# A chain of attention and four matrix layers: the first two matrix layers by one level of Strassen, attention of all batches ahead of them, and SBUF laid out by hand

## The chip, the cores and the metric

The kernel runs on one core of one Trainium2 chip. The metric is the device time in microseconds (us), the median of several runs. The engines in this text: PE is TensorE (matmul; PEld is its weight load), DVE is VectorE, ACT is ScalarE, POOL is GpSimd, SP is SyncE, whose queue issues every DMA here.

## The reference

```python
# q, k, v: 4 batches, 12 heads, 448 positions, 64 wide
scores = q @ k.T / sqrt(64) - log(448)
x = sigmoid(scores) @ v                        # per head; joined to 1792 x 768
h = maximum(maximum(x @ w1, x @ w2), x @ w3)   # layer 1, 768 to 768
y = h @ w_out                                  # layer 2, 768 to 768
m = y @ w_in                                   # layer 3, 768 to 2048
out = (m * sigmoid(1.702 * m)) @ w_out2        # layer 4, 2048 to 768
```

q, k and v are float32. The weights arrive as the bits of float64 numbers, and the kernel rounds them itself.

## The kernel before, in words

**Precision.** PE reads float32 operands in a rounded form (`F32R`). To keep precision, an operand is split: `hi` is the rounded copy, made by a cast (`copy`, L228), and `lo` is the rest, made by a subtraction on DVE (`rest`, which goes through `two`, L231). A product of two split operands takes three matmuls: hi by hi, hi by lo, lo by hi (L385 to L387). Every matmul of the four layers multiplies a weight block of 128 by 128 with 448 columns, the positions of one batch.

**Stages.** A *pair* is two heads of one batch; there are 24. `Pair` loads q and k in one piece (`t`, 488 KB) and splits them (`qh`, `ql`). Scores come in four chunks of keys (`score`): chunks 0 to 2 hold two heads at once, chunk 3 is one matmul wide. ACT applies the sigmoid (`scored`, L445). Then the scores are weighed with v: the first ten pairs (`PLAIN`) in plain float32 (`weigh_plain`, L484), the others with scores and v split (`weigh`, L465 and L469). `unit1` and `unit2` are layers 1 and 2 for one batch and one block of 128 outputs: 18 matmuls into one bank of PSUM. Their 24 weight tiles are made once (`new_weights`): a DMA of 768 KB (`raw`), an ACT operation (L342) and four DVE operations (L349, L353, L354, L358; from the ninth tile on ACT does the second one's work at L347) round the float64 bits to float32, then the split. They are stored split in DRAM (`kept`) and loaded again for batches 1 to 3. `unit3` and `unit4` are layers 3 and 4 in 8 groups of 256 of the 2048 columns.

**Order.** The code hands every operation to a planner (`Order`) with an estimated duration and the parts that it reads and writes. PE's order is nearly the order of the calls; the planner fixes each engine's queue, and it chooses for a copy between ACT and DVE. After eleven *beats* of attention the main loop mixes: for each unit of layers 1 and 2 of a batch it calls a beat of attention of the next batches, so that attention is spread over the first three batches. Layers 3 and 4 follow. Buffers are rings of tiles in pools.

Of the kernel before, what the change touches and what calls it, by code (L numbers as in the profile page):

```python
# [25 lines left out]
QK = Q + S  # L26

OFF = 48
# [3 lines left out]
PLAIN = range(10)  # L32

LOW_ACT = range(8, NW1)
# [6 lines left out]


MM, SWITCH = 0.201, 0.41

SLACK = 12.0

# [13 lines left out]
class Ring:  # L60


    def __init__(self, n, make):
        self.n, self.make, self.tiles = n, make, []

    def tile(self):
        t = Tile(self)
        self.tiles.append(t)
        return t


class Tile:
    def __init__(self, ring=None, get=None):
        self.ring, self.get, self.ap, self.ops = ring, get, None, []

    def __call__(self):
        if self.ap is None:
            self.ap = self.ring.make() if self.ring else self.get()
        return self.ap

    def part(self, cut=None):
        return Part(self, cut)


class Part:


    def __init__(self, tile, cut):
        self.tile, self.cut, self.writers, self.readers = tile, cut, [], []

    def __call__(self):
        ap = self.tile()
        return self.cut(ap) if self.cut else ap
# [8 lines left out]
class Order:  # L102

    def __init__(self):
        self.ops, self.rings, self.clock = [], [], 0.0

    def ring(self, n, make, gate=None):
        r = Ring(n, make)  # L110
        r.gate = gate
        self.rings.append(r)
        return r

    def op(self, on, fn, reads=(), writes=(), after=(), at=None, lag=0.1):
        o = Op(len(self.ops), on, fn, at, lag)
        self.ops.append(o)
        for p in reads:
            o.pre.update(p.writers)
        for p in writes:  # L120
            o.pre.update(p.readers)
            o.pre.update(p.writers)
        for p in reads:
            p.readers.append(o)
            p.tile.ops.append(o)
        for p in writes:
            p.writers.append(o)
            p.tile.ops.append(o)
        o.pre.update(after)
        o.pre.discard(o)  # L130
        return o
# [6 lines left out]
    def run(self):  # L138
        for r in self.rings:
            for old, new in zip(r.tiles, r.tiles[r.n :]):  # L140
                first = min(new.ops, key=lambda o: o.n)
                first.pre.update(x for x in old.ops if x is not first)
            for t in r.tiles if r.gate else ():
                min(t.ops, key=lambda o: o.n).pre.add(r.gate)
# [30 lines left out]
        while len(done) < len(self.ops):  # L175
            for e in free:
                while free[e] <= now + 1e-9 and ready[e]:
# [4 lines left out]
                    o.fn(e)  # L182
                    if e == "SP":
# [19 lines left out]

def moe_chain_kernel(tc, qk, vv, wa, wb, out):
# [5 lines left out]
    def pool(name, bufs=1, **kw):  # L210
        return tc.alloc_tile_pool(name=name, bufs=bufs, **kw)

    def ring(p, name, shape, n, dtype=F32, gate=None):
        return O.ring(n, lambda: p[0].tile(shape, dtype, name=name, tag=name, bufs=n), gate)


    def dma(to, of, kb, reads, writes):
        return O.op({"SP": kb / 330.0}, lambda e: sp.dma_start(to().bitcast(F32), of().bitcast(F32)), reads, writes)
# [5 lines left out]

# [8 lines left out]
    def rest(to, of, hi, n):  # L233
        return two(to, of, hi, ALU.subtract, n)


    base = [pool("base", side="left")]
    att = [pool("att", side="left")]
    xp = [pool("xp", side="right")]
    mid = [pool("mid", side="right")]  # L240
    xe = [pool("xe", side="right")]
    scratch = pool("scratch", space=bass.MemoryType.DRAM)
    pmm = [pool("pmm", space=PSUM)]
    patt = [pool("patt", space=PSUM)]
    late, acc, pout = [None], [None], [None]

    def to_late(e):
        att[0].release()
        xe[0].release()
        patt[0].release()  # L250
        late[0] = pool("late", side="left")
        late[0].tile([P, 8], F32, name="space")
        pout[0] = pool("pout", space=PSUM)

    def to_acc(e):
        mid[0].release()
        xp[0].release()
        acc[0] = pool("acc", side="right")

    raws = ring(base, "raw", [P, DM], 2, mybir.dt.uint64)  # L260
    ys = ring(base, "y", [P, DM], 3)
    att_rings = [
        ring(att, *a)
        for a in (
            ("t", [P, 1024], 2),
            ("qh", [P, 1024], 2, F32R),
            ("ql", [P, 1024], 2, F32R),
            ("a2", [P, 2, S], 5),
            ("a1", [P, S], 2),
            ("ah2", [P, 2, S], 4, F32R),  # L270
            ("ah1", [P, S], 2, F32R),
            ("al2", [P, 2, S], 4, F32R),
            ("al1", [P, S], 2, F32R),
            ("vf", [P, 7, D], 1),
            ("vs", [P, 14 * D + 64], 2, F32R),
            ("vp", [P, 7, D], 2),
            ("xf", [P, S], 2),
            ("fold", [D, S], 2),
        )
    ]  # L280
    ts, his, los, a2s, a1s, ah2s, ah1s, al2s, al1s, vfs, vss, vps, xfs, folds = att_rings
    xs = [[ring(p, f"x{k}", [P, 2, S], 1, F32R) for k in range(KC)] for p in (xe, xp)]
    w1s = ring(xp, "w1", [P, 2 * DM + 64], 4, F32R)
    hs = [ring(mid, f"h{k}", [P, 2, S], 1, F32R) for k in range(KC)]
    mxs = ring(mid, "mx", [P, S], 2)
    yst = ring(mid, "yst", [P, 2, S], 3, F32R)

    def banks(p, name, n, shape=(P, 512)):
        return O.ring(n, lambda: p[0].tile(list(shape), F32, name=name, tag=name, bufs=n))

    scs, avs, mms = banks(patt, "sc", 2, (P, 2, 512)), banks(patt, "av", 2), banks(pmm, "mm", 2)
    pos = banks(pout, "po", 6)
    w2s = ring(late, "w2", [P, 2 * DM + 64], 7, F32R)
    z0s = [ring(late, f"z{k}", [P, 2, S], 2, F32R) for k in range(KC)]
    zs = [ring(acc, f"z{k}", [P, 2, S], B - 2, F32R) for k in range(KC)]
    gs = ring(late, "g", [P, 4 * S], 2, F32R)
    sgs = ring(late, "sg", [P, S], 2)
    gfs = ring(late, "gf", [P, S], 2)
    accs = ring(acc, "acc", [P, S], B * KC)

    bias = base[0].tile([P, 1], F32, name="bias")
    nc.gpsimd.memset(bias, -math.log(S))
    warm = yst.tile().part()
    O.op({"-": 0.0}, lambda e: nc.gpsimd.memset(warm().bitcast(F32), 0.0), [], [warm])
    warmed = base[0].tile([P, 1], F32, name="warmed")
    act.activation(warmed, bias, AF.Sigmoid)

    def dram(name, shape):
        return Tile(get=lambda: scratch.tile(shape, F32R, name=name)).part()

    kept = [dram(f"kept{i}", [P, 2, DM]) for i in range(NW1)]
    ykept = [[dram(f"yk{b}_{k}", [P, 2, S]) for k in range(KC)] for b in range(B)]

    def bank(r):
        return r.tile().part(lambda a: a[:, :S])

    def split(r):

        t = r.tile()
        return t.part(lambda a: a[:, 0]), t.part(lambda a: a[:, 1]), t  # L320

    def weight_tile(r):
        t = r.tile()
        of = lambda n: t.part(lambda a: a[:, OFF + n * DM :][:, :DM])
        return of(0), of(1), Part(t, lambda a: a[:, OFF:][:, : 2 * DM].rearrange("p (t n) -> p t n", t=2))

# [9 lines left out]
    def new_weights(of, hi, lo, of_n):  # L336
        raw, y = raws.tile().part(), ys.tile().part()
        O.op({"SP": 768 / 330.0}, lambda e: sp.dma_start(raw(), of), (), [raw])
# [11 lines left out]

        e = "ACT" if of_n in LOW_ACT else "DVE"
        O.op({e: 1.95 if e == "ACT" else 1.02}, lambda _: low(e), [raw], [raw])
# [9 lines left out]
        copy(hi, y, DM)  # L362
        rest(lo, y, hi, DM)

    def weights1(b, i):
        hi, lo, t = weight_tile(w1s)
        if b == 0:
            new_weights(wa[i], hi, lo, i)
            dma(kept[i], t, 768, [hi, lo], [kept[i]])
        else:  # L370
            dma(t, kept[i], 768, [kept[i]], [hi, lo])
        return hi, lo

    def weights2(i):
        hi, lo, _ = weight_tile(w2s)
        new_weights(wb[i], hi, lo, NW1 + i)
        return hi, lo

    def product(ps, w, x):
        for k, (hi, lo) in enumerate(x):  # L380
            c = slice(k * P, (k + 1) * P)

            def f(_, k=k, c=c, hi=hi, lo=lo):
# [10 lines left out]
    class Pair:  # L394
# [58 lines left out]
        def weigh(self, c):  # L453

            if self.av is None:
                self.av = [bank(avs) for _ in range(2)]
# [312 lines left out]
```

## Time and profile before

| what | value |
|---|---|
| three timed runs | 975.25, 977.39, 979.49 us (median 977.39) |
| span of the profiled execution | 975.8 us |
| instructions of PE, DVE, ACT | 4930, 914, 489 |
| moved by DMA | 165.36 MB, mean 169 GB/s |

The profiled execution is one run, looked at instruction by instruction. Its span, from the first to the last instruction, is 975.8 us; no time of its own is listed beside it, so it is set against the median of the timed runs, which is 1.6 us more. Busy time of an engine is given in us and as a share of the span.

### The profile page before, as it was taken

How to read it: one execution, taken by the hardware profiler on the slowest of the kernel's cores; microseconds unless marked ns; L12 is line 12 of the kernel's file. 1: busy time of each engine (PE TensorE's matmuls, PEld its weight loads, DVE VectorE, ACT ScalarE, POOL GpSimd, SP SyncE). 2: the span in 40 equal slices, each digit the busy share in tenths (PEclk: the TensorE clock that was granted, in tenths of full speed). 3: DMA queues.
4: the chain of work that ended last, by engine and by line, in shares of the span. 5: the costliest groups of instructions: out<-in, count | busy, mean ns of one | idle time of the engine just before them, and what ended most of it. 6: DMA issues, size and time to landing. Idle time of an engine off the chain costs nothing.

```text
span 975.8 us, 12162 instructions
## 1 busy us (share of the span) xinstructions
PE 961.8 (99%) x4930; PEld 855.1 (88%) x4930; DVE 596.4 (61%) x914; ACT 349.6 (36%) x489; POOL 1.1 (0%) x6
## 2 busy tenths in 40 slices
PE   7899999999999999999999999999999999999998
PEld 4457788888888889989999999999999999999997
DVE  6768799996667621521642555777757576754344
ACT  6666799754445420211212431222222122121110
POOL 0000000000000000000000000000000000000000
PEclk9999999999999999999999999999999999999999
DMA  8858887975555656799985021110201112000023
GB/s 293 304 195 288 298 300 265 401 280 203 191 188 195 196 187 211 287 360 359 328 318 226 20 68 63 65 65 17 80 33 65 65 65 65 1 1 1 1 104 123
DMA packets 39656, 165.36 MB, mean 169 GB/s; under 512 B 4400, under 2 KB 11056, under 8 KB 39600
## 3 DMA queue, kind: packets, MB, share of 16 engines
q1 hardware_dynamic: 39600, 164.58, 47.3%
q8 instruction: 39, 0.64, 0.3%
q14 instruction: 17, 0.14, 0.0%
HBM read 129.17 MB, written 35.39 MB: 169 GB/s over the span
## 4 chain that ended last, share of the span: by engine, by line
PE 92%; DMA 4%; DVE 2%; ACT 1%; issue 1%; SPq 0%; DVEq 0%; ACTq 0%
PE mm L385 19%; PE mm L387 19%; PE mm L386 18%; PE po L643 8%; PE po L642 8%; PE po L641 8%; PE sc L435 4%; PE av L465 3%; DMA raw<-in_wa 3%; PE av L484 3%; PE sc L437 1%; DMA w<-kept 1%; PE av L469 1%; ACT a L445 0%; ACT y L342 0%
## 5 line engine op out<-in xcount | busy, mean ns | idle before, releaser
L385 PE MATMUL mm<-x,w 128*128 128x448 f32 x432 | 158.6, 367 | 0.0
L386 PE MATMUL mm<-x,w 128*128 128x448 f32 x432 | 156.8, 363 | 0.9 <-DVE x L231 0.9
L387 PE MATMUL mm<-x,w 128*128 128x448 f32 x432 | 156.7, 363 | 0.0
L231 DVE TENSOR_TENSOR acc<-po,acc 128x448 f32<-128x448 f32 (+1 forms) x169 | 104.8, 623 | 59.8 <-PE po L643 59.1
L643 PE MATMUL po<-g,w 128*128 128x448 f32 x384 | 139.4, 363 | 0.0
L387 PE MATMUL mm<-z,w 128*128 128x448 f32 x384 | 139.4, 363 | 0.0
L642 PE MATMUL po<-g,w 128*128 128x448 f32 x384 | 139.2, 362 | 0.0
L386 PE MATMUL mm<-z,w 128*128 128x448 f32 x384 | 139.2, 362 | 0.0
L385 PE MATMUL mm<-z,w 128*128 128x448 f32 x384 | 138.2, 360 | 0.0
L641 PE MATMUL po<-g,w 128*128 128x448 f32 x384 | 138.2, 360 | 0.0
L625 ACT ACTIVATE sg<-mm 128x448 f32<-128x448 f32 x64 | 34.9, 545 | 245.0 <-PE mm L387 245.0
L445 ACT ACTIVATE a<-sc,bias 128x896 f32<-128x896 f32 (+1 forms) x96 | 84.8, 914 | 48.6 <-PE sc L435 36.9
L385 PEld LDWEIGHTS mm<-x,w 128*128 128x128 f32 x432 | 80.9, 187 | 13.6 <-issue 7.1
L231 DVE TENSOR_TENSOR mx<-mm,mx 128x448 f32<-128x448 f32 x48 | 29.9, 624 | 95.5 <-PE mm L387 95.3
L231 DVE TENSOR_TENSOR gf<-mm,sg 128x448 f32<-128x448 f32 x64 | 40.1, 626 | 77.2 <-ACT sg L625 77.0
L386 PEld LDWEIGHTS mm<-x,w 128*128 128x128 f32 x432 | 81.1, 188 | 6.7 <-DVE x L231 1.2
L387 PEld LDWEIGHTS mm<-x,w 128*128 128x128 f32 x432 | 81.0, 188 | 5.0
L642 PEld LDWEIGHTS po<-g,w 128*128 128x128 f32 x384 | 72.1, 188 | 5.7
L386 PEld LDWEIGHTS mm<-z,w 128*128 128x128 f32 x384 | 72.1, 188 | 5.7
L641 PEld LDWEIGHTS po<-g,w 128*128 128x128 f32 x384 | 71.8, 187 | 5.0
L385 PEld LDWEIGHTS mm<-z,w 128*128 128x128 f32 x384 | 71.8, 187 | 5.0
L387 PEld LDWEIGHTS mm<-z,w 128*128 128x128 f32 x384 | 72.1, 188 | 3.8
(78 smaller groups left out, 1334.2 us busy)
## 6 DMA issues: line engine op xcount, KB each, us to landing
w<-kept SPq DMA_DIRECT2D x72, 768.0 KB, 4.9
raw<-in_wb SPq DMA_DIRECT2D x32, 768.0 KB, 5.1
raw<-in_wa SPq DMA_DIRECT2D x24, 768.0 KB, 5.7
kept<-w SPq DMA_DIRECT2D x24, 768.0 KB, 5.3
t<-in_qk SPq DMA_DIRECT2D x23, 488.0 KB, 5.1
yk<-yst SPq DMA_DIRECT2D x24, 448.0 KB, 7.9
z<-yk SPq DMA_DIRECT2D x24, 448.0 KB, 7.3
out_t<-acc SPq DMA_DIRECT2D x23, 224.0 KB, 1.9
```

The lines of the kernel that those rows point to most:

```text
L231: return on("DVE", t_two(n), lambda: dve.tensor_tensor(to(), a(), b(), op=op), [a, b], [to])
L385: pe.matmul(ps(), wh[:, c], xh, start=k == 0, stop=False)
L386: pe.matmul(ps(), wh[:, c], lo(), start=False, stop=False)
L387: pe.matmul(ps(), wl[:, c], xh, start=False, stop=k == KC - 1)
L435: pe.matmul(o[:, e, :], kx[r, keys], qx[r, Q:QK], **how)
L445: on("ACT", t_act(n) + 0.07, lambda: act.activation(a(), ps(), AF.Sigmoid, bias=bias, scale=scale), [ps], [a])
L465: pe.matmul(av[e](), w, x()[:, e, :], start=c + n == 0, stop=False)
L484: pe.matmul(o[r], w, xe, start=c == 0, stop=c == 3)
L625: on("ACT", t_act(S), lambda sg=sg, ps=ps: act.activation(sg(), ps(), AF.Sigmoid, scale=1.702), [ps], [sg])
L641: pe.matmul(ps(), wh[:, c], gh, start=j == 0, stop=False)
L642: pe.matmul(ps(), wh[:, c], gl, start=False, stop=False)
L643: pe.matmul(ps(), wl[:, c], gh, start=False, stop=j == 1)
```

## The change

Five things change together.

**Strassen.** For layers 1 and 2 two batches are taken together, and the product is cut into blocks of two by two: weights into four quarters (`a11` to `a22`, 384 by 384), the moving side into half of the features by batch (`b11` to `b22`). Seven products (`product`, 9 matmuls each) replace eight, in Winograd's form. `moving` makes the seven moving operands by four subtractions (`combine`) and seven splits (`fill`); `Weights` makes the seven weight operands by four additions or subtractions and seven splits, in the first round only; the second round loads them from DRAM (`kept`, 384 KB each). A `Set` holds the seven products for one weight: three PSUM banks, in which sums grow, one ACT copy from bank to bank, two ACT copies to SBUF, and additions on the way out (`put`). `stage` interleaves the sets: step n of set i stands at 7i + 2n.

**Attention.** All 24 pairs come first, and all are weighed in plain float32. One weight tile is rounded per pair (`prepare`) and stored to DRAM as one float32 (`yk`, 384 KB); `LOW_ACT` is empty, so all four rounding operations stay on DVE.

**x, h and z** are kept as float32, and split where they are used. z of two batches goes through DRAM at 224 KB a piece.

**SBUF** is three slabs (`r`, `f`, `m1`, later `m2`) with fixed places, and dependencies by ranges of columns. **PSUM** is one tile of eight banks, handed out in turn.

```diff
-PLAIN = range(10)
-
-LOW_ACT = range(8, NW1)
+LOW_ACT = ()
...
+        def fill(self, base, cuts=((0, 2), (2, 1))):
+            for j, n in cuts:
+                split(self.parts(0, j, n), self.parts(1, j, n), F(base + j * T, n * T), n * T)
+
+        def pair(self, j):
+            return self.parts(0, j, 1), self.parts(1, j, 1)
+
+    def moving(base):
+        b11, b12, b21, b22, t = (base + 3 * i * T for i in range(5))
+        cuts = ((0, 2), (2, 1))
+
+        def combine(to, x, y):
+            for j, n in cuts:
+                sub(*(F(z + j * T, n * T) for z in (to, x, y)), n * T)
+
+        m = {k: Moving() for k in ("b11", "t1", "t2", "b21", "t3", "b22", "t4")}
+        m["b11"].fill(b11)
+        combine(t, b12, b11)
+        m["t1"].fill(t)
+        combine(b11, b22, t)
+        m["t2"].fill(b11)
+        m["b21"].fill(b21)
+        combine(b12, b22, b12)
+        m["t3"].fill(b12)
+        m["b22"].fill(b22)
+        combine(b21, b21, b11)
+        m["t4"].fill(b21)
+        return [m[k] for k in ("b11", "t1", "t2", "b21", "t3", "b22", "t4")]
...
+                y, s = yp_at(), s_at()
+                dma(F(y, 2 * DM), yk[i][0], 768)
+                q = [(y + n * HW) for n in range(4)]
+                self.s = [s + n * HW for n in range(4)]
+                a11, a12, a21, a22 = q
+                s1, s2, s3, s4 = self.s
+                self.steps = [
+                    (a11, None),
+                    (s1, (add, s1, a21, a22)),
+                    (s2, (sub, s2, s1, a11)),
+                    (a12, None),
+                    (s3, (sub, s3, a11, a21)),
+                    (s4, (sub, s4, a12, s2)),
+                    (a22, None),
+                ]
+
+        def operand(self, n):
+            at = w_at()
+            hi, lo, both = R(at + OFF, HW), R(at + OFF + HW, HW), R(at + OFF, 2 * HW)
+            k = kept[self.i][n]
+            if not self.first:
+                dma(both, k, 384)
+                return hi, lo
+            src, how = self.steps[n]
+            if how:
+                how[0](*(F(x, HW) for x in how[1:]), HW)
+            split(hi, lo, F(src, HW), HW)
+            dma(k, both, 384)
+            return hi, lo
...
+        O.pe(f, 9 * MM, [*w, *(z for p in parts for z in p)] + ([] if fresh else [ps]), [ps])
...
+        def step(self, n):
+            if n == 0:
+                self.w = self.weights()
+                self.a, self.b, self.e = (banks(ps_at()) for _ in range(3))
+            name = ("a", "e", "b", "a", "b", "e", "b")[n]
+            ps = getattr(self, name)
+            product(ps, self.w.operand(n), self.x[n], n < 2)
+            if n == 0:
+                copy(self.b, ps, S, psum=True, both=False)
+            elif n == 1:
+                self.m5 = temp()
+                copy(self.m5, ps, S, psum=True, both=False)
+            elif n == 2:
+                self.u2 = temp()
+                copy(self.u2, ps, S, psum=True, both=False)
+            elif n == 3:
+                self.put(0, 0, ps, None)
+            elif n == 4:
+                self.put(1, 1, ps, self.m5)
+            elif n == 5:
+                self.put(0, 1, ps, self.u2)
+            else:
+                self.put(1, 0, ps, None)
+
+    def stage(sets):
+        for _, s, n in sorted((7 * i + 2 * n, i, n) for i in range(len(sets)) for n in range(7)):
+            sets[s].step(n)
...
+        def weigh(self):
+            b, hp = divmod(self.p, NPAIR)
+            ps, v, a = banks(7), self.v, self.a
...
+                        wv, xe = (w[:, 2 * c + e], x[:, e * S : (e + 1) * S]) if c < 3 else (w[r, 6], x[r, :])
+                        pe.matmul(o[r], wv, xe, start=c == 0, stop=c == 3)
+
+            O.pe(f, 4 * 0.75 + SWITCH, [v, *a], [ps])
+            half, j = divmod(hp, HK)
+            base = XA if b < 2 else XB
+            copy(F(base + (6 * half + 3 * (b % 2) + j) * T, S), ps, S, psum=True)
...
+    def prepare(k):
+        for i, n, t in singles[k : k + 1]:
+            y = F(y_at(), DM)
+            single(wa[t], y, "DVE")
+            dma(yk[i][1](n), y, 384)
+
+    prev = None
+    for p in range(NP):
+        c = Couple(p)
+        if p == 0:
+            c.score(0, slice(0, 1))
+            c.score(1, slice(0, 1))
+            c.score(0, slice(1, 3))
+            c.score(1, slice(1, 3))
...
+            c.score(0)
+            c.score(1)
+        c.score(2)
+        c.score(3)
+        if prev:
+            prev.weigh()
+        prev = c
+        prepare(p)
+    prev.weigh()
...
+    def layer1(x, first):
+        sets = []
...
+                sets.append(Set(x, lambda m=m, e=e: Weights(3 * m + e, first), put))
+        stage(sets)
...
+    x = moving(XA)
+    for tp in range(2):
+        layer1(x, tp == 0)
+        h = moving(XA)
+        layer2(h, tp == 0, tp)
+        if tp == 0:
+            x = moving(XB)
+            for b in range(2):
+                for k in range(KC):
+                    dma(F(zf_at[b] + k * T, T), zk[b][k], 224)
...
-    for b in range(B):
-        first = at
-        for n, (layer, m, e) in enumerate(order):
-            while b < B - 1 and at < min(beats, first + -(-9 * (n + 1) // (17 if b else 22))):
-                beat(at)
-                at += 1
-            if (b, n) == (B - 1, len(order) - 1):
-                break
```

On PE, in the middle of attention, the rows before are these (`sc` are scores, `av` the weighed result, `vp` v, `mm` a bank of layer 1, `a` the sigmoids).

```order
L435 MATMUL sc<-qh,ql 128x448 x2
L484 MATMUL av<-a_568,vp 64x448 x2
L484 MATMUL av<-a_570,vp 64x448 x2
L484 MATMUL av<-a_594,vp 64x448 x2
L484 MATMUL av<-a_615,vp 64x448 x2
L437 MATMUL sc<-qh 128x448
L437 MATMUL sc<-ql,qh 128x448
L437 MATMUL sc<-qh,ql 128x448
L385 MATMUL mm<-x_308,w_313 128x448
L386 MATMUL mm<-x_308,w_313 128x448
```

At the end of attention the changed kernel has these on PE (L521 and L523 are scores, L550 weighs, L438 is a product of layer 1; `r`, `f`, `m` are the slabs, `ps` is PSUM).

```order
L521 MATMUL ps<-r 128x448 x18
L523 MATMUL ps<-r 128x448 x3
L550 MATMUL ps<-m_73,f 64x448 x8
L521 MATMUL ps<-r 128x448 x18
L523 MATMUL ps<-r 128x448 x3
L550 MATMUL ps<-m_73,f 64x448 x8
L438 MATMUL ps<-r 128x448 x9
L550 MATMUL ps<-m_73,f 64x448 x8
L438 MATMUL ps<-r 128x448 x558
```

No product stands between the scores of the pairs any more, and the first product of layer 1 stands ahead of the last weighing.

SP's queue in the middle of attention holds loads of q and k, of v and of `raw`, and stores of the split weights, in loose order before:

```order
L338 DMA raw<-in_wa 128x768
L412 DMA vp<-in_vv 128x448
L218 DMA kept_782<-w_749 128x1536
L338 DMA raw<-in_wa 128x768
L218 DMA kept_826<-w_801 128x1536
L404 DMA t<-in_qk 128x976
```

Now it repeats four DMAs per pair.

```order
L268 DMA f<-in_qk 128x976
L268 DMA f<-in_vv 128x448
L320 DMA f<-in_wa 128x768
L262 DMA yk_580<-f 128x768
L268 DMA f<-in_qk 128x976
L268 DMA f<-in_vv 128x448
L320 DMA f<-in_wa 128x768
L262 DMA yk_664<-f 128x768
```

The load of `raw` (L320) now stands behind the load of v, and the load of the next q and k behind the store of the rounded weight.

On DVE at the seam from layer 1 to layer 2 of the first round the changed kernel has these (L280 is every two-operand operation, L277 a cast or copy; `m_1272` is the slab `m2`, which holds the first moving operands of layer 2).

```order
L280 TENSOR_TENSOR f<-f 128x448
L280 TENSOR_TENSOR m_1272<-f,m_1272 128x896
L280 TENSOR_TENSOR f<-f 128x896
L280 TENSOR_TENSOR r<-f,r 128x384
L280 TENSOR_TENSOR f<-ps,f 128x448
L280 TENSOR_TENSOR f<-f 128x896
```

Two thirds of each moving operand (896 of 1344 columns) are made while layer 1 still runs; the last third follows when its last set is done.

## Rows read from the trace of the kernel before

**Rows 1.** The page's first part: busy time, share of the span, instructions.

```profile
PE 961.8 (99%) x4930; PEld 855.1 (88%) x4930; DVE 596.4 (61%) x914; ACT 349.6 (36%) x489; POOL 1.1 (0%) x6
```

**Rows 2.** Windows: stretch, its length, busy us (count) by engine, clock, DMA share, GB/s.

```profile
25.00:50.00 25.00, 21.59 (x115) 11.86 (x112) 18.08 (x26) 14.53 (x18) 0.00 (x0) 0.93 0.86 298
...
100.00:150.00 50.00, 49.49 (x257) 40.71 (x255) 43.65 (x65) 41.63 (x44) 0.00 (x0) 1.00 0.84 302
...
400.00:450.00 50.00, 48.92 (x245) 45.49 (x244) 19.88 (x30) 9.83 (x15) 0.00 (x0) 1.00 0.96 351
...
600.00:700.00 100.00, 100.00 (x502) 93.75 (x501) 70.25 (x113) 24.21 (x38) 0.00 (x0) 1.00 0.13 48
```

**Rows 3.** Timeline of PE: the first matmul of layer 3, the last of layer 4.

```profile
506.90 0.36 PE L385 MATMUL mm<-z,w 128*128 128x448 f32 x1
...
971.70 0.37 PE L643 MATMUL po<-g,w 128*128 128x448 f32 x1
```

**Rows 4.** The chain that ended last, 60 to 75 us: start, us, what.

```profile
61.34 1.41 PE sc L435 x12
...
67.98 3.31 PE av L484 x16
71.29 0.82 PE sc L437 x3
72.10 0.20 PE mm L385
```

**Rows 5.** Groups by line and shape, ACT: busy us, mean ns, idle before.

```profile
L445 ACT ACTIVATE a<-sc,bias 128x896 f32<-128x896 f32 x72 | 70.1, 1007 | 37.7 <-PE sc L435 36.9 <-PE av L484 0.5
...
L445 ACT ACTIVATE a<-sc,bias 128x448 f32<-128x448 f32 x24 | 15.2, 634 | 10.8 <-PE sc L437 10.7
...
L342 ACT ACTIVATE y<-raw 128x768 f32<-128x768 f32 x56 | 50.8, 913 | 50.8 <-DVE w L231 22.1 <-DMA raw<-in_wa 17.5 <-DMA raw<-in_wb 10.0
...
L228 ACT CAST x<-av 128x448 fp32r<-128x448 f32 x5 | 2.7, 533 | 6.3 <-PE av L484 6.3
```

**Rows 6.** Groups by line and shape, DVE.

```profile
L358 DVE SCALAR_TENSOR_TENSOR y<-raw,y 128x768 uint32<-128x768 uint32 x56 | 53.0, 959 | 1.0 <-ACT raw L347 0.3
...
L231 DVE TENSOR_TENSOR al<-a,ah 128x896 fp32r<-128x896 f32 x42 | 45.0, 1086 | 0.1
L349 DVE TENSOR_SCALAR raw<-raw 128x768 uint16<-128x768 uint16 x40 | 40.6, 1048 | 0.0
...
L353 DVE TENSOR_SCALAR y<-y 128x768 f32<-128x768 f32 x56 | 31.1, 557 | 9.7 <-ACT y L342 8.9
...
L354 DVE TENSOR_SCALAR y<-y 128x768 uint32<-128x768 uint32 x56 | 31.0, 566 | 0.1
L231 DVE TENSOR_TENSOR mx<-mm,mx 128x448 f32<-128x448 f32 x48 | 29.9, 624 | 95.5 <-PE mm L387 95.3
...
L231 DVE TENSOR_TENSOR ql<-t,qh 128x976 fp32r<-128x976 f32 x23 | 26.9, 1170 | 0.1
...
L228 DVE CAST qh<-t 128x976 fp32r<-128x976 f32 x14 | 9.3, 665 | 4.9 <-PE sc L437 4.8
```

**Rows 7.** Tile `raw`, 60 to 160 us: from issue to landing.

```profile
DMA to landing us min/median/max: 4.2/5.6/8.4
```

**Rows 8.** Timeline of ACT: the first two sigmoids.

```profile
7.29 1.90 ACT L445 ACTIVATE a<-sc,bias 128x896 f32<-128x896 f32 x2
```

**Rows 9.** Groups by line and shape: a copy out of PSUM by ACT.

```profile
L228 ACT COPY mx<-mm 128x448 f32<-128x448 f32 x14 | 7.6, 540 | 34.7 <-PE mm L387 34.7
```

**Rows 10.** Timeline of PE around a wait: start, us, what, idle time before.

```profile
38.28 0.48 PE L437 MATMUL sc<-qh 128*128 128x448 f32 x1 [2.00 <-ACT a L445]
...
41.23 0.58 PE L435 MATMUL sc<-ql,qh 64*128 64x448 f32 x2
41.61 0.58 PE L435 MATMUL sc<-qh,ql 64*128 64x448 f32 x2
42.12 4.16 PE L484 MATMUL av<-a,vp 128*64 128x448 f32 x16
```

More of the change, by code (lines that the diff above doesn't have):

```diff
@@ L245, in moe_chain_kernel @@
[L245 to L280, printed above, removed]
@@ L311, in moe_chain_kernel @@
[L311 to L325, printed above, removed]
+    XA, XB = 0, 15 * T
@@ L423, in score @@
[L423 to L430 removed]
+                tp, hp, lp = F(t + c.start, n), R(h + c.start, n), R(l + c.start, n)
+                load(tp, qk[p][:, c], n / 2)
+                copy(hp, tp, n)
+                sub(lp, tp, hp, n)
@@ new lines, in moe_chain_kernel, with put @@
+    prev.weigh()
+    gate[0] = O.op({"-": 0.0}, to_m2, after=set(s1.ops))
+    def layer1(x, first):
+        sets = []
+        for m in range(HK):
+            for e in range(3):
+                def put(half, tok, ps, other, m=m, e=e):
+                    to = F(XA + (6 * half + 3 * tok + m) * T, S)
+                    if e == 0 and other is None:
+                        copy(to, ps, S, psum=True)
+                        return
+                    if other is not None:
+                        new = to if e == 0 else temp()
+                        add(new, ps, other, S)
+                        ps = new
+                    if e:
+                        two(to, ps, to, ALU.max, S)
+                sets.append(Set(x, lambda m=m, e=e: Weights(3 * m + e, first), put))
+        stage(sets)
@@ new lines, in moe_chain_kernel, with layer2, put @@
+    zk = [[dram(f"z{b}_{k}", [P, S])[0] for k in range(KC)] for b in range(2)]
+    zf_at = [XB + 6 * T * b for b in range(2)] + [XA + 6 * T * b for b in range(2)]
+    def layer2(h, first, tp):
+        sets = []
+        for m in range(HK):
+            def put(half, tok, ps, other, m=m):
+                k = m + HK * half
+                to = temp() if tp == 0 else F(zf_at[2 + tok] + k * T, T)
+                if other is None:
+                    copy(to, ps, S, psum=True)
+                else:
+                    add(to, ps, other, S)
+                if tp == 0:
+                    dma(zk[tok][k], to, 224)
+            sets.append(Set(h, lambda m=m: Weights(9 + m, first), put))
+        stage(sets)
@@ L606, in moe_chain_kernel, with weights2 @@
+    w2_at = Round([WREG + i * 1600 for i in range(5)])
+    assert WREG + 5 * 1600 <= RW
+    def weights2(i):
+        at = w2_at()
+        y = F(y_at(), DM)
+        single(wb[i], y, "ACT" if i < 0 else "DVE")
+        hi, lo = R(at + OFF, DM), R(at + OFF + DM, DM)
+        split(hi, lo, y, DM)
+        return hi, lo
     NG = NF // 2
```

571 lines of the change are left out of this document (245 added, 326 removed).

## The prediction

> **What bounds the kernel now.** I read the page's busy shares first. PE is busy for 961.8 of 975.8 us, DVE for 61%, ACT for 36% [rows 1]. The windows say whether one engine holds this throughout. In 600 to 700 us PE is busy for all of 100.00 us at the full clock and DVE for 70.25; in 100 to 150, where attention and layer 1 are mixed, PE has 49.49 of 50, and DVE 43.65 and ACT 41.63 are close behind; only in 25 to 50 does PE show gaps (21.59 of 25) with a mean clock of 0.93 [rows 2]. So the end is set by the number of matmuls, except in the first 50 us. The timeline gives the price of one: from the first matmul of layer 3 at 506.90 to the last of layer 4 at 971.70 [rows 3] there are 2304 of layers 3 and 4 and the 18 of layer 2's last unit, so 2321 steps in 464.8 us, 0.2003 us each.
>
> From 506.90 to the end of the span are 468.9 us; less those 18 (3.6) layers 3 and 4 with the tail are 465.3. The other 1710 matmuls of layers 1 and 2 are 342.5. What is left, 975.8 - 468.9 - 342.5 = 164.4, is start, attention and waits.
>
> **Fewer products.** Layers 1 and 2 need 12 sets of 7 products of 9 matmuls, twice: 1512 in place of 1728. At 0.2003 that is 302.8 in place of 346.1: 43.3 us less, on the engine that is never idle there.
>
> **Attention by itself.** One pair on PE: two chunks of scores 1.41, the third 0.60 (three steps of 0.20), the narrow fourth 0.82, the plain weighing 3.31 [rows 4]: 6.14 us. The same pair asks of ACT three wide sigmoids, a narrow one, the first rounding step and the copy of x out of PSUM: 3 x 1.007 + 0.634 + 0.913 + 0.533 = 5.10 [rows 5]. Of DVE it asks the cast and rest of q and k and four rounding steps: 0.665 + 1.170 + 1.048 + 0.557 + 0.566 + 0.959 = 4.97 [rows 6]. Meanwhile x of the first two batches is made ready: 7 rests and 4 combinations, each 896 and 448 columns wide, 11 x (1.086 + 0.624) = 18.8 us of DVE [rows 6], some 0.85 per pair, and at most 7 x (1.007 + 0.634) = 11.5 of ACT, 0.5 per pair. So PE 6.14, DVE 5.8, ACT 5.6: PE still sets it, by little. DMA moves 488 + 224 + 768 + 384 = 1864 KB (1.91 MB) per pair, 311 GB/s at 6.14; the row of 100 to 150 has 302 at a share of 0.84 and that of 400 to 450 has 351 at 0.96 [rows 2], so a share of about 0.86.
>
> What may be slower is the chain of the weight tiles. Only two `raw` buffers exist, so a tile's load, ACT's step and DVE's four repeat every two pairs: 5.6 to land (median; up to 8.4) [rows 7], 0.91, 3.13, and in DVE's queue one cast and rest of q and k between them, 1.84: 11.5, or 14.3 with the slowest load, so 5.75 to 7.15 per pair before any waiting in the queues. SP's queue couples it to the pairs, since the next q and k wait behind `raw` and the store. PE's 6.14 is the floor; I take 6.4, near it: at this DMA share most loads should land as in the window of rows 7, a few late.
>
> The sum of the stage: ACT's first sigmoid starts at 7.29 [rows 8], as before, since the same loads come first; the first pair's sigmoids take 3.66, then come the second pair's last chunk (0.8) and the first weighing at a low clock (4.1, rows 10 have 4.16): 15.9. From there to the end of pair 22's weighing are 22 rounds of 6.4: 140.8, so 156.7. Then layer 1 needs its first operand. Before it stand the last tiles' steps on ACT and DVE, the store of tile 21, the load of the first rounded pair of tiles and a split. At 6.14 per pair, pair 21 starts at 15.9 + 19 x 6.14 = 132.6, its sigmoids end 0.6 + 3.66 later, and the copy of x, ACT's step and DVE's four take 0.53 + 0.91 + 3.13: 141.4. With 5.6 for the store and 5.6 for the load (both taken like `raw`) and 1.2 for the split that is 153.8, against PE free at 15.9 + 22 x 6.14 = 151.0: a wait of some 3, which moves with the pace. Then the last weighing, 3.4. Together 163.1, about what start, attention and waits take now (164.4): the plain weighing costs PE 3.31 against 14 steps of 0.20 for the split one, 0.5 more on 14 pairs, and DVE and ACT lose the splits of the sigmoids.
>
> **Seams and the first round of Strassen.** Per set DVE has 4 combinations and 7 rests of 384 columns, at most 0.624 each (the 448 row, [rows 6]), 6.9, and in layer 1 on average 4.7 exits of 0.624, 2.9: at most 9.8 in the 63 x 0.2003 = 12.6 us that PE needs. ACT has 3 copies of 0.54 [rows 9] and 7 casts of at most 0.634: 6.1. So PE sets the pace inside a layer. The copy from bank to bank has no row; the nearest is 0.54 out of PSUM [rows 9]. It must be done within one product, 1.8 us; from nothing to 1.8 it costs nothing, and I take nothing. Without that cover each 0.1 us would cost 24 x 0.1.
>
> At the seam to layer 2 the last thirds of the moving operands remain, 11 operations of 0.624. After the last product of layer 1 some six stand before the second operand (3.7 us) and PE has one product (1.8): 2 us, in each round. Layer 2 of round one also has to make x for round two: DVE needs 3 x 8.1 + 6.9 + 18.8 = 50 us, and PE gives 37.9 plus 12.6 of the next set: no room, so I put 4 there. The second set's weights wait for the store and load of the last tile, 11.2 us, with four products and a weighing (10.6) to cover it: 2. Together 10. The lower end is 2, if the planner's order hides all; the upper is 27, if at four seams nothing is hidden (4 x 6.9).
>
> The second round loads its 84 operands of 384 KB in some 155 us, 213 GB/s, under the rates above: nothing. Layers 3 and 4 keep their matmuls. They add 8 splits of z, 13.7 us of DVE, in the first groups, where DVE has some 30% free [rows 2]: nothing; without cover 13.7.
>
> **Sum.** 163.1 + 302.8 + 10 + 465.3 = 941.2 us of span. The profiled span stands 1.6 below the median of the runs shown, so **943**.
>
> One rule of the Trainium skill speaks against the change: "Perfetto Trace Analysis", section "Optimization Strategy", advises interleaving regimes with different bottlenecks, and the change takes apart what was interleaved. By it the attention stage should no longer run at PE's pace. The windows agree that the mixed stretch kept PE at 99% [rows 2]; by the sums above attention alone still leaves PE the longest, so I follow the sums and let the rule stand behind the first rival.
>
> **The rivals.**
> First, *the weight tiles set the pace of attention*: 7.0 to 7.6 per pair in place of 6.4, if loads land at 8 us. That is 22 x 0.6 to 1.2, 13 to 26 more: 956 to 969. For it: two buffers only, one in-order queue. Against it: the median landing. Its far end is the case on the other side: at 8.0 per pair, a chain of 16 us, the gain is gone, and each 1 us beyond costs 22; that asks for loads of over 9 us, beyond any in rows 7, or the ACT step queued behind a whole pair's sigmoids. At 8.5 the time is 989.
>
> Second, *nothing is lost*: 6.14 per pair, no wait at the end, seams of 2: 15.9 + 135.1 + 3.4 + 302.8 + 2 + 465.3 = 924.5, so 926.
>
> Third, *DVE sets the pace of round one*: if its queue order makes it wait on PE, 2 to 3 us more per set on 12 sets, 967 to 979.
>
> Fourth, *the clock falls in attention*. After 2.00 us of waiting the matmuls of a score came 0.38 apart, which is the lower of the clock's two levels (1.2 against 2.4 GHz), and the weighing took 4.16 in place of 3.31 [rows 10, 4], about 1.8 us lost each time. If every pair had such a wait it would be 22 x 3.5: 1020. In "TensorE: Matmul & The Clock Gate", section "The HAM clock gate", the skill says that the throttled clock is the default and activity releases it; the trace agrees with its 0.93 in the stretch with gaps [rows 2]. PE's queue in attention has no such gap if ACT's 5.6 fits under 6.14, so I give it little.
>
> That Strassen saves nothing is excluded by rows 1 and 3: matmuls stand back to back.
>
> **Chances.** Forecast (930 to 955) 0.60; nothing lost (922 to 930) 0.13; weight tiles up to 969 0.13, beyond 0.04; DVE in round one 0.06, half of it within 0.5% of now; clock 0.04. Under 0.5% (some 5 us) a measurement cannot tell a change from none. Faster by more: 0.60 + 0.13 + 0.12 + 0.03 = 0.88; within it 0.05; slower 0.07. The range for 8 in 10 is 924 to 967.
>
> **What would show it.** PE's matmuls fall by 216 in layers 1 and 2, with steps of 0.20 there. Weighings of attention come 6.1 to 6.7 apart; if they come at 7 or more, and ACT's first rounding step waits for `raw`, the first rival is right. The first product starts at 155 to 163. At the seams PE waits for rests by DVE, 2 to 4 us each. Layers 3 and 4 take 465 us. The prediction is wrong if attention ends after 170 or PE shows waits inside the sets.

## The result, and the profile after

The changed kernel takes 934.05 us (median; 933.24 to 935.65) beside 976.32 (973.67 to 979.49) for the kernel before on the same chip: a ratio of 0.957, 95% interval 0.9546 to 0.9594. The forecast was 943. The profiled execution is one of 933.24 us, with a span of 931.4.

The page's first part answers [rows 1]: PE has 216 matmuls less and is as full as it was.

```profile
PE 918.9 (99%) x4714; PEld 792.3 (85%) x4714; DVE 624.7 (67%) x987; ACT 351.9 (38%) x564; POOL 1.1 (0%) x6
```

All waits of PE in the changed kernel (what it waited for, us in total, times, longest) come to some 9 us, and only 3.6 of them stand at a product (L438):

```profile
PE ps L438 <- ACT r L277: 3.6, 1, 3.6
PE ps L566 <- POOL r L560: 1.7, 1, 1.7
PE ps L550 <- ACT f L277: 1.4, 1, 1.4
PE ps L521 <- ACT m L534: 1.0, 2, 0.8
PE ps L550 <- DVE f L277: 0.9, 1, 0.9
PE ps L521 <- DVE r L280: 0.3, 1, 0.3
```

The windows (columns as in [rows 2]) show attention at 15 to 156, the end of it, and the first sets of round one. DVE and ACT are high in attention but PE is higher; behind 167 PE has no gap, and DVE is busy 44.31 of 63.

```profile
15.00:60.00 45.00, 44.67 (x277) 22.87 (x277) 39.04 (x53) 34.51 (x46) 0.00 (x0) 1.00 0.84 295
60.00:110.00 50.00, 46.77 (x276) 22.37 (x274) 44.58 (x62) 40.17 (x53) 0.00 (x0) 1.00 0.83 286
110.00:156.00 46.00, 45.38 (x269) 21.63 (x265) 35.98 (x51) 34.10 (x45) 0.00 (x0) 1.00 0.87 301
156.00:167.00 11.00, 7.77 (x29) 4.29 (x30) 7.52 (x14) 4.25 (x10) 0.00 (x0) 0.84 0.62 246
167.00:230.00 63.00, 63.00 (x317) 59.05 (x316) 44.31 (x86) 27.55 (x57) 0.00 (x0) 1.00 0.91 319
```

PE's timeline has the weighings (L550), the first scores of a slow round, the first product (L438), and the first and last matmul of layers 3 and 4 (as [rows 3]):

```profile
42.88 3.38 PE L550 MATMUL ps<-m,f 128*64 128x448 f32 x16
49.00 3.38 PE L550 MATMUL ps<-m,f 128*64 128x448 f32 x16
...
61.25 3.38 PE L550 MATMUL ps<-m,f 128*64 128x448 f32 x16
65.39 2.67 PE L521 MATMUL ps<-r 64*128 64x448 f32 x18 [0.76 <-ACT m L534]
67.99 0.87 PE L523 MATMUL ps<-r 128*128 128x448 f32 x3
68.97 3.38 PE L550 MATMUL ps<-m,f 128*64 128x448 f32 x16
...
152.25 3.38 PE L550 MATMUL ps<-m,f 128*64 128x448 f32 x16
159.23 3.81 PE L438 MATMUL ps<-r 128*128 128x448 f32 x9 [3.61 <-ACT r L277]
162.97 3.38 PE L550 MATMUL ps<-m,f 128*64 128x448 f32 x16
...
465.19 0.36 PE L690 MATMUL ps<-r 128*128 128x448 f32 x1
...
927.59 0.37 PE L716 MATMUL ps<-m,r 128*128 128x448 f32 x1
```

An ordinary round, weighing to weighing, is 6.12 us (42.88 to 49.00). Five of the 22 are longer, by 5.9 us together: the first by 0.6, behind a wait for DVE's rest of q and k, the other four by 5.3; that of 61.25 takes 7.72. ACT's timeline says why there: the first rounding step (L324) waits 4.46 us for a raw tile, and the sigmoids (L534), whose scores are there, stand behind it in ACT's queue.

```profile
58.55 0.53 ACT L277 COPY f<-ps 128x448 f32<-128x448 f32 x1
63.54 0.90 ACT L324 ACTIVATE f<-f 128x768 f32<-128x768 f32 x1 [4.46 <-DMA f<-in_wa]
64.34 3.31 ACT L534 ACTIVATE m<-ps,bias 128x896 f32<-128x896 f32 x4
```

ACT waits for raw tiles six times in the stage, 17.0 us in all. What held this load back stands in the chain that ended last: DVE's last step on an earlier tile (L339) frees the buffer, and only then is the load issued.

```profile
54.44 0.97 DVE f L339
55.47 8.00 DMA f<-in_wa
```

For raw tiles the row that answers to [rows 7] (20 to 160 us, issue to landing) is a little later than before:

```profile
DMA to landing us min/median/max: 4.9/6.5/8.0
```

From the second product on (166.28, behind the last weighing) 765.1 us remain to the end of the span. That number is the measure of the experiments: what they change lies before that matmul or behind it.

### The profile page after: what moved, and what is told of

It is laid out like the page before. It is cut to its first block, busy times and chain, and to the rows that moved or that the text cites. A ratio compares the mean times of both kernels' runs of the same rounds, so it can differ in the third digit from the quotient of the medians.

```text
span 931.4 us, 12177 instructions
## 1 busy us (share of the span) xinstructions
PE 918.9 (99%) x4714; PEld 792.3 (85%) x4714; DVE 624.7 (67%) x987; ACT 351.9 (38%) x564; POOL 1.1 (0%) x6
## 4 chain that ended last, share of the span: by engine, by line
PE 83%; DMA 7%; DVE 6%; ACT 3%; issue 1%; SPq 0%; DVEq 0%; ACTq 0%
PE ps L438 33%; PE ps L716 8%; PE ps L692 8%; PE ps L691 8%; PE ps L715 8%; PE ps L714 8%; PE ps L690 8%; DMA f<-in_wa 4%; ACT m L534 2%; DMA f<-in_qk 2%; DVE r L280 1%; DVE f L339 1%; DMA yk<-f 1%; DVE f L331 1%; DVE r L277 1%
## 5 line engine op out<-in xcount | busy, mean ns | idle before, releaser
L280 DVE TENSOR_TENSOR f<-ps,f 128x448 f32<-128x448 f32 x305 | 188.0, 623 | 197.0 <-ACT f L696 76.4
L438 PE MATMUL ps<-r 128*128 128x448 f32 x1242 | 254.9, 364 | 3.6 <-ACT r L277 3.6
L438 PEld LDWEIGHTS ps<-r 128*128 128x128 f32 x1242 | 233.7, 188 | 21.3 <-ACT r L277 4.4
L280 DVE TENSOR_TENSOR r<-f,r 128x384 fp32r<-128x384 f32 (+4 forms) x246 | 179.5, 745 | 19.3 <-ACT r L277 16.2
L277 ACT CAST r<-f 128x384 fp32r<-128x384 f32 (+3 forms) x178 | 104.5, 609 | 97.7 <-DVE f L280 32.9
L277 ACT COPY f<-ps 128x448 f32<-128x448 f32 x113 | 60.4, 535 | 131.3 <-PE ps L438 106.3
L692 PE MATMUL ps<-r 128*128 128x448 f32 x288 | 104.5, 363 | 0.0
L716 PE MATMUL ps<-r 128*128 128x448 f32 x288 | 104.5, 363 | 0.0
L691 PE MATMUL ps<-r 128*128 128x448 f32 x288 | 104.4, 362 | 0.0
L715 PE MATMUL ps<-r 128*128 128x448 f32 x288 | 104.4, 362 | 0.0
L690 PE MATMUL ps<-r 128*128 128x448 f32 x288 | 103.7, 360 | 0.0
L714 PE MATMUL ps<-r 128*128 128x448 f32 x288 | 103.7, 360 | 0.0
L550 PE MATMUL ps<-m,f 128*64 128x448 f32 (+1 forms) x384 | 81.0, 551 | 2.4 <-ACT f L277 1.4
L534 ACT ACTIVATE m<-ps,bias 128x896 f32<-128x896 f32 x96 | 79.8, 924 | 1.8 <-PE ps L521 1.8
L280 DVE TENSOR_TENSOR f<-f 128x384 f32<-128x384 f32 (+2 forms) x104 | 66.5, 661 | 11.6 <-DMA f<-yk 11.2
L324 ACT ACTIVATE f<-f 128x768 f32<-128x768 f32 x56 | 51.1, 920 | 47.9 <-DVE r L280 22.9
L277 DVE CAST r<-f 128x976 fp32r<-128x976 f32 (+5 forms) x68 | 37.1, 550 | 45.9 <-PE ps L691 24.6
L550 PEld LDWEIGHTS ps<-m,f 128*64 128x64 f32 (+1 forms) x384 | 23.2, 135 | 49.1 <-issue 44.4
L331 DVE TENSOR_SCALAR f<-f 128x768 uint16<-128x768 uint16 x56 | 58.2, 1040 | 0.0
L438 PE MATMUL ps<-m,r 128*128 128x448 f32 x270 | 58.2, 362 | 0.0
L715 PEld LDWEIGHTS ps<-r 128*128 128x128 f32 x288 | 54.0, 188 | 4.2
```

Of the source, the lines that this page charges most:

```text
L277: return O.op(engines, lambda e: (act.copy if e == "ACT" else dve.tensor_copy)(to(), of()), [of], [to])
L280: return on("DVE", t_two(n), lambda: dve.tensor_tensor(to(), a(), b(), op=op), [a, b], [to])
L331: dve.tensor_scalar(half(2), half(1), 13, None, op0=ALU.logical_shift_right)
L438: pe.matmul(o, a[:, c], b, start=fresh and j == n == 0, stop=j == HK - 1 and n == 2, skip_group_check=True,)
L534: lambda: act.activation(to(), ps(), AF.Sigmoid, bias=bias, scale=scale),
L550: pe.matmul(o[r], wv, xe, start=c == 0, stop=c == 3)
```

## The experiments

Each run is compared with the changed kernel's 934.05 us; the ratio given is to the kernel before.

**Eight products.** The sets of layers 1 and 2 get the plain four blocks, two products each; attention, rounding and slabs stay.

```diff
-        for ... in sorted((7 * i + 2 * n, i, n) ... for n in range(7)):
+        for ... in sorted((8 * i + 2 * n, i, n) ... for n in range(8)):
-            name = ("a", "e", "b", "a", "b", "e", "b")[n]
-            product(ps, self.w.operand(n), self.x[n], n < 2)
+            half, k, tok = n // 4, n // 2 % 2, n % 2
+            product(self.c[tok], self.op, self.x[2 * k + tok], k == 0)
```

> Eight block products in place of seven in layers one and two, attention first and slabs as in the changed kernel. Theory (PE sets the pace everywhere, and the 216 matmuls that are gone are the whole gain): 216 x 0.2003 us come back, so 934 + 43 = 977 us, within 0.4% of the kernel before, and PE has no wait over 1 us at the seams. Rival 1 (attention apart, or the layout, gave part of the gain): 965 to 972. Rival 2 (attention apart costs, and the seven products gave more than their matmuls): 982 or more.

974.86 us (ratio 0.9983, interval 0.9969 to 0.9997): 40.8 more. The timeline splits it. The stretch behind the last weighing goes from 765.1 to 971.4 - 162.81 = 808.6, 43.5 more, the 216 steps. Ahead of it 3.5 us go, since the first weight operand is there in time and no gap opens.

```profile
162.81 12.48 PE L421 MATMUL ps<-r 128*128 128x448 f32 x60
```

So the theory holds, and all else that the change did (attention apart, plain weighing, slabs) comes to 0.2% with eight products.

**All weighings plain in the kernel before.**

```diff
-PLAIN = range(10)
+PLAIN = range(24)
```

> The kernel before, with all 24 batch pairs weighed in plain float32 instead of the first ten. Theory (PE sets the pace in the mixed rounds too): 14 weighings each about 0.5 us longer on PE, 7 us more, 981 to 985. Rival (the mixed rounds lose time on ScalarE and VectorE, which split the weights there, and plain weighing is part of the gain): 976 or less.

983.3 us (ratio 1.0086, interval 1.0064 to 1.0107), 7.0 more: the theory's number, and PE's busy time rises by 6.9, from 961.8 to 968.7. With e1_eight it says that the rest of the change beside Strassen (attention apart, the slabs, where x, h, z and the rounding lie) costs nothing together; it gives back about what the plain weighing takes. What each part does by itself is not shown.

**The raw loads cut short.**

```diff
+        k = slice(0, DM if loads[0] <= 2 or loads[0] > 24 else 96)
-        ... sp.dma_start(raw().bitcast(mybir.dt.uint64), of) ...
+        ... sp.dma_start(raw().bitcast(mybir.dt.uint64)[:, k], of[:, k]) ...
```

> In the attention stage each load of a raw weight tile brings one eighth of its bytes after the first two (the rest of the tile keeps what was there, so the output isn't the reference's); every instruction stands where it did. Theory (the five slow rounds, 5.9 us over the 22, come from raw tiles that land late, with ScalarE's first rounding step waiting ahead of the sigmoids): rounds of 6.12 throughout and an earlier first product, 5 to 9 us less, 925 to 929. Rival 1 (the slow rounds come from ScalarE's and VectorE's own work, 37 to 45 us of 50): 932 to 934. Rival 2 (they come from the stores of the rounded tiles and the loads of queries, keys and values): 931 to 934, with the waits then on these transfers.

922.58 us (ratio 0.9453, interval 0.9428 to 0.9479): 11.5 less, more than expected, since the gap before layer 1 went too. The rounds now take 6.12, but for the first (6.46). So the late raw tiles are the cause of the other slow rounds; ACT's and DVE's own work, which stayed, did not keep them slow. The shorter loads also bring the DMA share between 15 and 156 from 0.85 to 0.60, so this run does not part a buffer that comes free late from transfers that are slow; the next one does.

**Four raw buffers, three raw buffers.** Two slots of the moving ring lie in the slab that holds the sigmoids first, and that space takes two more raw buffers during attention.

```diff
-slots = [i * SLOT for i in range(7)] + [RW, RW + SLOT]
+slots = [i * SLOT for i in range(5)] + [RW + i * SLOT for i in range(4)]
...
+    raw_more = Round([F(a, 2 * DM) for a in raw_at.places]
+                     + [M1(14 * T + i * 1536, 2 * DM) for i in range(2)])
...
-        raw = F(at, 2 * DM)
+        raw = raw_more() if loads[0] <= 24 else F(raw_at(), 2 * DM)
```

> Four buffers for raw weight tiles in the attention stage instead of two (the two more lie in the slab of the sigmoids, made larger by two slots of the moving ring); order of the matmuls after attention as before. Theory (a tile of raw weights is late because its buffer comes free late): rounds of 6.12 and 4 to 7 us less, 927 to 930. Rival (the transfers themselves are the limit in that stage, 84% of the DMA engines' time): slow rounds remain, 932 to 934.

923.32 us (ratio 0.9462, interval 0.944 to 0.9483), 10.7 less, the fastest kernel here that computes the whole reference. Its PE has one wait in attention, of 0.77, and its timeline at the end of the stage shows rounds of 6.12 and the first product behind the weighing without a gap:

```profile
141.54 3.38 PE L552 MATMUL ps<-m,f 128*64 128x448 f32 x16
144.84 2.08 PE L523 MATMUL ps<-r 64*128 64x448 f32 x18
146.86 0.88 PE L525 MATMUL ps<-r 128*128 128x448 f32 x3
147.66 3.38 PE L552 MATMUL ps<-m,f 128*64 128x448 f32 x16
150.97 2.07 PE L440 MATMUL ps<-r 128*128 128x448 f32 x9
152.97 3.38 PE L552 MATMUL ps<-m,f 128*64 128x448 f32 x16
156.28 11.08 PE L440 MATMUL ps<-r 128*128 128x448 f32 x54
```

Behind 156.28 are 921.4 - 156.28 = 765.1 us, as in the changed kernel. Raw tiles land no sooner in this kernel (its page; KB each, median us to landing):

```profile
f<-in_wa SPq DMA_DIRECT2D x12, 768.0 KB, 7.0
m<-in_wa SPq DMA_DIRECT2D x12, 768.0 KB, 8.0
```

Against 6.6 in the changed kernel's page the medians are later, and ACT's rounding step waits for none. Between 15 and 156 the DMA engines move 329 GB/s, against 294. So the transfers were not the limit; that a load had to wait for one of two buffers was.

With `range(1)` in place of `range(2)` there are three:

> Three raw buffers instead of two (e10_raw4 had four). Theory (a buffer is held for the landing, 6 to 8 us, and the rounding, some 4 us, so a third already lets a round take 6.12): 923 to 925, like four buffers. Rival (four were needed): 926 to 930, with slow rounds left.

927.37 us (ratio 0.9498, interval 0.9473 to 0.9524): the rival's range. The trace keeps slow rounds, with one wait of 1.2 us on ACT's copy; three buffers get about two thirds of the gain of four.

**The weighing first, and another place for the last tiles.** Two edits on the 3.6 us gap before the first product. The first makes that product wait for the last weighing on PE; the second lets tiles 20 to 23 take two of the four places of the ring, so that the places of the first pair read back come free earlier.

```diff
+            first_after[0] = O.pe(f, 4 * 0.75 + SWITCH, [v, *a], [ps])      # weigh
...
-        O.pe(f, 9 * MM, [...], [ps])
+        O.pe(f, 9 * MM, [...], [ps], after)
```

> The last weighing is put ahead of the first product of layer one on PE; nothing else is meant to move. Theory: the weighing fills the 3.6 us in which PE waited for the first weight operand, the granted clock does not fall, and the first nine matmuls take 1.8 us and not 3.8; 3 to 5 us less, 929 to 931. Rival: the second operand (a sum on DVE and its split) is late in any case, so PE waits there: 1 us less at most, 933 to 934.

931.91 us (ratio 0.9552, interval 0.9537 to 0.9566), 2.1 less, between the two. The chain that ended last in this kernel shows the store of tile 21, then the load into its place, then ACT:

```profile
148.43 3.66 DMA yk<-f
...
152.15 5.22 DMA f<-yk
...
157.39 0.03 ACT r L277
...
157.81 0.53 ACT f L277
...
158.39 5.07 PE ps L554 x16
```

ACT waits for that load at the cast of the weight operand, and behind the cast stands the copy that frees the weighing's bank. So the weighing waits for the same load by another way, 2.97 us, and then takes 5.07 in place of 3.38; from 159 to 162 us the granted clock is 0.50.

```diff
-            y = F(y_at(), DM)
+            y = F(y_at.places[k % 4 if k < 20 else 2 + k % 2], DM)
```

> The last four rounded tiles use two of the four places of their ring, so that the first pair of tiles read back for layer one no longer waits until the tile before last is stored. Theory (the 3.6 us wait before the first product, and the low clock behind it, come from that place alone): the load is issued some 10 us earlier, the first operand is there when attention ends, the gap and the slow first product go: 4 to 6 us less, 928 to 930. Rival (two places for the last four tiles delay their rounding, or VectorE has no time for the operand): 932 to 935, the wait then on VectorE.

927.41 us (ratio 0.9503, interval 0.9478 to 0.9529), 6.6 less. The first product follows the weighing at once, in 2.08 us in place of 3.81. By the profiled spans it is 4.4 less, all of it ahead of the last 765.1 us. The weighing behind that product now waits 0.74. So the gap came from that place, which comes free late. Another place is not the only cure: e10_raw4 and e6_short_raw leave the places as they were, their raw tiles do not come late, and no gap opens there either.

**A rounding step back on ACT.**

```diff
-            single(wa[t], y, "DVE")
+            single(wa[t], y, "DVE" if k < 8 else "ACT")
```

> The changed kernel with one rounding step of the raw tiles from the ninth on put back on ScalarE (1.95 us there, 1.03 us on VectorE). Theory (ScalarE then has 5.2 + 1.95 = 7.1 us of work in a round of 6.1 to 6.4 and sets the pace): 11 to 16 us more, 945 to 950. Rival (casts and evictions that may run on either engine go to VectorE instead, and ScalarE keeps 6.2 us a round): 934 to 938.

933.44 us (ratio 0.9556, interval 0.9528 to 0.9585): no difference that can be measured. My theory fell, and the rival's mechanism is there: between 15 and 156 us ACT's casts drop from 12 to 4 and its copies from 20 to 8, which DVE takes, and ACT's busy time rises by 11.6 us only. The move of this step, part of the change, is worth nothing here.

**The seams.** The moving operands made in one piece, with the changed kernel's attention and then with four raw buffers:

```diff
-        def fill(self, base, cuts=((0, 2), (2, 1))):
+        def fill(self, base, cuts=((0, 3),)):
...
-        cuts = ((0, 2), (2, 1))
+        cuts = ((0, 3),)
```

> The moving operands of each layer are made in one piece of three tiles, not in two tiles and then one. Theory (the seams cost nothing because two thirds of each operand are made ahead, and only one tile's work stands behind the last set): PE waits 1 to 3 us for the second or third operand at each of the two seams into layer two, 2 to 6 us more, 936 to 940. Rival (the three products left in the last set are cover enough whatever the cut): 934 as before, no wait over 0.5 us.

> e10_raw4 with the moving operands made in one piece of three tiles: the seams by themselves, since with four raw buffers the attention stage has no stalls that could move. Theory (e4_whole's 7.1 us more were the seams): 5 to 7 us above e10_raw4, 928 to 930, waits at the seams into layer two alone. Rival (half of e4_whole's loss was the end of the attention stage): 2 to 4 us more, 925 to 927.

941.13 us (ratio 0.9646, interval 0.9624 to 0.9668), 7.1 more; and with four buffers 931.6 (0.9537, interval 0.9513 to 0.9561), 8.3 above e10_raw4 (9.1 by the spans), both more than their theory gave. The second product of layer 1 divides them: from it on are 6.6 us more than the 765.1 in the first and 930.5 - 160.49 = 770.0, 4.9 more, in the second. The 1.7 between them stand behind the second seam, where PE waits 1.80 in both: in e4_whole the granted clock is 0.50 behind it (440 to 442 us), in e13_raw4_whole it stays at 1.00. In e13_raw4_whole the other 4.2 lie in attention, where around 42 us ACT's rounding step waited twice for a store to free its place (1.94 and 1.90 us), the copy that frees a weighing's bank stood behind it, and PE idled 2.72. The waits stand at the two seams into layer 2, and nowhere else in layers 1 and 2 (timeline of PE in e13_raw4_whole; a fifth, of 0.25, is at 424.43):

```profile
270.95 5.68 PE L440 MATMUL ps<-m,r 128*128 128x448 f32 x27 [0.17 <-DVE m L280]
277.43 3.68 PE L440 MATMUL ps<-m,r 128*128 128x448 f32 x17 [0.80 <-DVE m L280]
...
285.30 10.87 PE L440 MATMUL ps<-r 128*128 128x448 f32 x53 [0.39 <-DVE r L280]
...
431.90 3.68 PE L440 MATMUL ps<-r 128*128 128x448 f32 x17 [1.80 <-DVE r L280]
```

What in the planned order hides them was the last question: at the seam into layer 2 of round one the planner puts set two's first product and set one's fourth, both ready early, ahead of set one's second.

```diff
...
+            after = third if n in (0, 3) else []
-            product(ps, self.w.operand(n), self.x[n], n < 2)
+            o = product(ps, self.w.operand(n), self.x[n], n < 2, after)
+            if n == 2 and not third:
+                third.append(o)
...
```

> e10_raw4, in which the first three products of each layer's first set stand ahead of the first product of the second set and of the fourth product (in the changed kernel the planner puts these two, whose operands are ready early, between the first product and the second). Theory (these two products, 3.6 us of PE, are what hides the last third of the second operand at the seams into layer two): PE waits 1 to 3 us for a rest by VectorE at each of these two seams, 2 to 6 us more than e10_raw4, 925 to 929. Rival (the two-thirds cut alone is enough): 923 to 924, no wait there.

924.11 us (ratio 0.9469, interval 0.9456 to 0.9482), 0.8 more than e10_raw4 and no wait of a product listed: the rival. In this kernel's timelines, PE and then DVE, the 36 matmuls from 264.75 are the last two products of layer 1, then the first and second of layer 2. They take 0.4 us more than 36 steps.

```profile
264.75 7.76 PE L440 MATMUL ps<-m,r 128*128 128x448 f32 x36
272.36 3.76 PE L440 MATMUL ps<-r 128*128 128x448 f32 x18
```

```profile
266.75 0.62 DVE L280 TENSOR_TENSOR f<-ps,f 128x448 f32<-128x448 f32 x1
...
267.76 0.62 DVE L280 TENSOR_TENSOR f<-f 128x448 f32<-128x448 f32 x1
...
269.10 1.62 DVE L280 TENSOR_TENSOR f<-f 128x448 f32<-128x448 f32 x3
270.63 0.62 DVE L280 TENSOR_TENSOR r<-f,r 128x448 fp32r<-128x448 f32 x1
271.17 0.62 DVE L280 TENSOR_TENSOR m<-f,m 128x448 fp32r<-128x448 f32 x1
```

The quarter that the second operand needs leaves the product before the last (ends at 266.55); its maximum is the first row, its combination with the first quarter the second, its rest the last, done at 271.79. Only the rest of the last tile comes so late, and a product reads that in its eighth matmul, which starts at 271.84. Until then PE has the last product of layer 1, the first of layer 2 and seven steps of the second, 1.8 + 1.8 + 1.4 = 5.0 of the 5.2 us.

**One product fewer.**

```diff
-            product(ps, self.w.operand(n), self.x[n], n < 2)
+            w = self.w.operand(n)
+            if n != 4:
+                product(ps, w, self.x[n], n < 2)
```

> The fifth product of each set of layers one and two is left out (216 matmuls fewer, so the output isn't the reference's); its operands are still made, stored and read, and all sums on VectorE stay. Theory (PE is still what bounds these layers, with VectorE busy 44 us in 63 in the first set): 43 us less, 889 to 893. Rival (VectorE's or ScalarE's sums and splits, or the 90% busy DMA engines, are close behind and bind in round one): 25 to 38 us less, 896 to 909, with PE waits inside the sets of round one.

895.39 us (ratio 0.9173, interval 0.914 to 0.9206; runs from 891.83 to 898.11), 38.7 less: at the border of the two. The profiled run is the fastest of them, 41.4 us below the changed kernel by the spans. Behind its first product PE now waits five times, 3.5 us in all: four times in round one (2.75 us, for ACT's and DVE's operands, 1.09 at most) and once, 0.75, for a load of `kept`, which stands in round two. So at six products PE still sets nearly all of the time, but the others are close; what the slower runs lose besides is not shown.

## Why the prediction was right, and where its size was off

The mechanism held: the gain is 216 matmuls at 0.20 us, and attention apart costs about what it did mixed. By the sum's terms:

- **Start and attention**: 163.1 foretold. The second pair's last chunk and the first weighing end at 14.96 (15.9; the weighing took 3.38, at the full clock). The 22 rounds end at 155.56, 6.39 each (6.4). The wait is 3.61 (3), and the product behind it 1.9 us slower at a granted clock of 0.84 in that window, which I had not counted. Less the first product's ordinary 1.8 the stage ends at 164.5, 1.4 late.
- **1512 products**: 302.8 foretold. From 164.5 to layer 3's first matmul at 465.19 are 300.7 us, in which 1503 stand (nine of the last set come later), 0.2001 each.
- **Seams**: this is the step that failed. I put 10: 2 at each seam into layer 2, 4 at x for round two and 2 at the second set's weights. The steps above leave nothing for any of them: 0.0. "After the last product of layer 1 some six stand before the second operand (3.7 us) and PE has one product (1.8)" had the wrong start and too little cover: the operand hangs on the product before the last, and only its last tile is late, the rest of which PE reads after seven steps of the product. Hence 5.0 of cover, even without the two products that the planner puts there (e14_strict). For x in round two I had "no room", 50 us of DVE in 50.5; the rows below show DVE busy for 34.71 in the 38 us of layer 2, and for 13.41 in the 38 behind it. The lower end, "if the planner's order hides all", was the place to stand; the 2/1 cut carries it (4.9 us more without, 6.6 where the clock fell), the order of the products gives at most 0.8. What covers the second set's weights no run takes apart.

```profile
280.00:318.00 38.00, 38.00 (x192) 35.62 (x191) 34.71 (x57) 22.69 (x43) 0.00 (x0) 1.00 0.79 300
318.00:356.00 38.00, 38.00 (x192) 35.61 (x191) 13.41 (x21) 8.38 (x16) 0.00 (x0) 1.00 0.96 329
```

- **Layers 3, 4 and the tail**: 465.3 foretold; from 465.19 to the end are 466.2, less nine steps 464.4.

So 931.4 against 941.2: +1.4 in the first stage, -10.3 in the products with their seams, -0.9 behind them.

Of the rivals, the first (weight tiles) was there in four rounds of 22, 5.3 us or 0.24 per round over the floor, not 0.9 to 1.5: two buffers do bind, and four take it away. The end of attention had the same kind of cause, a place in a ring freed by a store. Of the second, "nothing lost", the seams came true, and e10_raw4 gives the rest: 923.3 against its 926. The third and fourth rivals show nothing: no wait inside the sets, and the windows' clock is 1.00 in attention. The rule of the Trainium skill on interleaving ("Perfetto Trace Analysis", "Optimization Strategy") did not decide here: taken apart, attention still ran at PE's pace but for the raw buffers, so the most contended engine stayed the same. With eight products the kernel with attention apart took 974.86 us beside 976.27 for the mixed one.

## What to carry to other kernels

When PE is full, fewer matmuls are worth their steps, if every engine's work per round is still under PE's; price that sum first. Price a seam by the product on which the late operand really hangs, and by the tile of it that is read last. Where a transfer ends a wait, look at what held its issue back: two more buffers gave 10.7 us although the median load then landed later.

## What was not expected of the hardware

- DVE's operations in a row start closer than they last: three of 448 columns take 1.62 us together where one is shown with 0.62, and the next starts 1.53 behind the first, so some 0.51 to 0.54 each. My sums with 0.624 each were some 15 to 20% high.
- One queued instruction of ACT that waits for a load costs PE more than its wait: after 3.61 us of idling the first nine matmuls took 3.81 in place of 2.08, and after 2.97 a weighing took 5.07 in place of 3.38. The granted clock was 0.50 there (160 to 162 us in the changed kernel, 159 to 162 in e2_order), the lower of its two levels (1.2 GHz, the upper 2.4). After 0.74 in e8_places a weighing took its 3.38, and after 1.80 at the second seam the clock was 0.50 in e4_whole and 1.00 in e13_raw4_whole. A longer time after a short wait need not be the clock: after 0.76 a set of scores took 2.67 in place of 2.08 at a granted clock of 1.00 (65 to 68 us).
